# Strassen's scheme for the projection of four of twelve tiles: seven half-size products in place of eight

## The chip, the cores and the metric

The kernel runs on one NeuronCore of a Trainium2 chip. The metric is the device time of one execution in microseconds. Five engines run side by side, each with its own instruction queue: TensorE (PE, matmuls), VectorE (DVE), ScalarE (ACT), GpSimd (POOL) and SyncE (SP, which issues most DMAs). The profile's name PEld is PE's weight load, which overlaps its matmuls.

## The reference

Two steps. First attention over 4 sequences, 8 heads, 768 positions and 64 dimensions a head; some heads ("retrieval") see the whole causal past, the others a window of 64 positions and 4 sinks. Then a feed-forward layer over the 3072 resulting tokens:

```python
def _moe_ref(x, w_in, w_out) -> np.ndarray:
    h = x @ w_in              # 3072 x 512 @ 512 x 2048
    g = h - np.tanh(h)
    return (g @ w_out).astype(np.float32)   # 3072 x 2048 @ 2048 x 512
```

`x` is the attention's output with its heads side by side. Inputs and output are fp32.

## The kernel before

**Tiles.** The 3072 tokens are 12 tiles of 256 (`TT`); tiles 0 to 2 are sequence 0, and so on. Each tile goes through attention, then H (times `w_in`, tanh shrink), then O (the projection, times `w_out`). Products are fp16 with fp32 sums in the PSUM banks, of which there are eight.

**Attention.** Inputs are loaded as fp32 (`load_raw`), POOL casts and sorts the heads (`gather`, lines 641 and 677), DMAs transpose q and k, PE computes scores (`st_S`, line 1069), ACT takes the exponential (line 1082), DVE masks it (`mask`, lines 1105 and 1133), PE multiplies by v (`st_A`, line 1162), DVE normalises (line 1194), and one DMA transposes the tile into `xT` (`st_X_tile`, line 1226). In `mask`, the heads of a "near" pair (tile `ptn`) take two multiplications of 512 elements, one for each head.

**H.** `H_unit(t, u)` makes two of the 16 blocks of 128 of the hidden layer: 8 matmuls of 256 columns (line 1273) into one bank, the tanh on ACT (line 1285), and on DVE the difference, scaled, into the fp16 tile `gt` (line 1292). Eight units make a tile. There are three `gt` buffers.

**O.** `O_group` multiplies 128 tokens by `w_out`: 16 matmuls of 512 columns that sum over the 16 hidden blocks (line 1331), so 32 matmuls a tile. `store` copies the bank out on ACT (line 1305; for one half of the last tile on DVE, line 1309) and sends it (line 1317), two stores of 256 KB a tile.

**Order.** The instructions are not issued as the code writes them. Each `op(engine, ns, fn, r, w)` is recorded with a price and with keys that it reads and writes; `Plan.run` simulates the engines with these prices and issues the instructions in the simulated order, the earliest recorded first among those that are ready. A flag `port=True` marks DVE instructions that the plan delays while POOL is at work. The recording order comes from `slots`: one slot for each H unit, with a piece of the projection of the tile before, and attention steps, loads (`LD`), gathers (`GA`) and masks spread over the slots by the tables `CUT`, `CUT1` and by `spread_over`. For tiles from `QUART` = 7 on, the projection of the tile before stands in two whole groups, at units 3 and 7. After the last tile's H come its two groups of O, the second cut into two halves of 256 columns, on two queues.

`program(True)` is what runs; `program(False)` is a second version that only runs when more than four heads are retrieval heads, which isn't so here.

## Time and profile before

| | |
|---|---|
| Time of the runs | 231.74 us median of 3 (231.14 to 231.82) |
| Profiled execution, first to last instruction (span) | 229.3 us; what lies around it is 2.4 us against the median of the runs (its own whole time is not listed apart) |
| O on PE, line 1331 | 464 matmul records, 304 of 512 and 160 of 256 columns |
| H on PE, line 1273 | 768 matmuls of 256 columns |
| DVE busy | 143.7 us, of it 65.1 in line 1292, 12.7 in line 1105, 12.1 in line 1133 |
| ACT busy | 141.7 us, of it 57.3 in line 1285, 15.1 in line 1305 |
| POOL busy | 98.2 us, all of it before 155 us |
| HBM | 27.26 MB read, 6.29 MB written |

The first tanh of tile 6 begins at 124.1 us of the span, of tile 8 at 159.8, of tile 9 at 173.0, of tile 10 at 189.5, of tile 11 at 205.3; the last matmul ends at 225.25.

In the profile a line such as L1331 is a line of the kernel's file. A group's busy time is the union of its instructions, so that the mean of one, times the count, can be more. Matmuls are pipelined: a record's length is longer than the step from one to the next. The chain that ended last is followed back from the last instruction, at each step to what released it.

### The profile page before, as it was taken

What the parts mean: (1) busy time and instruction counts of PE and PEld (TensorE: products, weight loads), DVE (VectorE), ACT (ScalarE), POOL (GpSimd) and SP (SyncE); (2) the same over time, 40 slices, a digit from 0 to 9 for tenths busy, and PEclk for the clock granted to TensorE, in tenths of its full rate; (3) what the DMA queues carried; (4) which work ended last, traced back from release to release, by engine and by line L of the source; (5) the groups of instructions that cost most, each with busy time, mean ns of one, the idle gap of its engine ahead of it and who ended that gap; (6) DMA issues with size and microseconds to landing.
All of it is one profiled execution on the core that took longest, in us unless ns stands there. A gap on an engine that the chain in (4) does not pass through costs nothing.

```text
span 229.3 us, 6150 instructions
## 1 busy us (share of the span) xinstructions
PE 220.8 (96%) x2335; PEld 158.2 (69%) x2335; DVE 143.7 (63%) x350; ACT 141.7 (62%) x219; POOL 98.2 (43%) x231
## 2 busy tenths in 40 slices
PE   7889999999999999999999999999999999999992
PEld 7456687788986667767667668756857757766662
DVE  5888957875676956749655759467876546634400
ACT  3739839977477757736737757755767567433420
POOL 8999343764843839391827773370000000000000
PEclk9999999999999999999999999999999999999999
DMA  6999999999999999989999999953121301320112
GB/s 171 151 181 203 202 192 222 218 185 243 222 179 232 168 245 218 187 199 229 239 192 278 181 210 166 212 124 95 54 40 46 92 3 46 73 55 15 49 67 78
DMA packets 102964, 35.31 MB, mean 154 GB/s; under 512 B 90642, under 2 KB 100114, under 8 KB 102930
## 3 DMA queue, kind: packets, MB, share of 16 engines
q1 hardware_dynamic: 85632, 27.14, 57.0%
q0 software_dynamic: 17152, 7.60, 25.5%
q8 instruction: 19, 0.31, 0.6%
q14 instruction: 15, 0.12, 0.2%
q10 hardware_dynamic: 146, 0.13, 0.2%
HBM read 27.26 MB, written 6.29 MB: 146 GB/s over the span
## 4 chain that ended last, share of the span: by engine, by line
PE 79%; DMA 9%; POOL 5%; ACT 3%; DVE 1%; issue 1%; SPq 0%; POOLq 0%
PE banks L1331 35%; PE banks L1273 32%; DMA win<-in_moe_w_in_dram 7%; PE banks L1162 6%; PE banks L1069 6%; DMA rawqk<-in_k_dram 2%; POOL v L495 2%; ACT pt L1082 1%; POOL win L608 1%; POOL t16p L528 1%; ACT QK L955 1%; POOL A L742 0%; DVE pt L1123 0%; ACT th L1285 0%; DVE ptn L1105 0%
## 5 line engine op out<-in xcount | busy, mean ns | idle before, releaser
L1331 PE MATMUL banks<-wout,gt 128*128 128x512 f16 (+1 forms) x464 | 94.9, 343 | 0.0
L1273 PE MATMUL banks<-xT,win 128*128 128x256 f16 x768 | 93.9, 273 | 0.6 <-DVE gt L1292 0.5
L1292 DVE SCALAR_TENSOR_TENSOR gt<-th,banks 128x512 f16<-128x512 f32 x96 | 65.1, 682 | 31.3 <-ACT th L1285 30.4
L1273 PEld LDWEIGHTS <-win 128*128 128x128 f16 x768 | 73.1, 98 | 16.6 <-issue 1.7
L1285 ACT ACTIVATE th<-banks 128x512 f32<-128x512 f32 x96 | 57.3, 603 | 36.4 <-PE banks L1273 35.8
L1331 PEld LDWEIGHTS <-gt 128*128 128x128 f16 x464 | 42.4, 98 | 27.4 <-issue 1.2
L1082 ACT ACTIVATE pt<-banks 128x768 f16<-128x768 f32 (+1 forms) x60 | 53.0, 922 | 11.0 <-PE banks L1069 10.6
L641 POOL CAST t<-rawqk 128x256 f16 x72 | 28.6, 446 | 31.6 <-DMA rawqk<-in_k_dram 26.8
L1305 ACT ACTIVATE ot<-banks 128x512 f32<-128x512 f32 (+1 forms) x28 | 15.1, 538 | 24.2 <-PE banks L1331 23.5
L1194 DVE TENSOR_TENSOR x16t<-banks,rinv 128x128 f32 (+1 forms) x80 | 22.6, 287 | 1.6
L1105 DVE TENSOR_TENSOR ptn<-ptn,mS 128x512 f16<-128x512 f16 x24 | 12.7, 567 | 16.2 <-ACT ptn L1082 16.2
L1069 PE MATMUL banks<-QK 64*128 64x128 f16 (+1 forms) x364 | 21.0, 238 | 0.8 <-ACT QK L955 0.8
L677 POOL CAST v<-rawv 128x128 f16 x72 | 19.6, 322 | 0.0
L1069 PEld LDWEIGHTS <-QK 64*128 64x128 f16 x364 | 12.6, 94 | 10.0 <-issue 7.2
L1082 ACT ACTIVATE ptn<-banks 128x1024 f16<-128x1024 f32 (+1 forms) x18 | 17.1, 950 | 3.5 <-DVE x16t L1194 2.4
L1162 PEld LDWEIGHTS <-pt 128*128 128x128 f16 x420 | 16.0, 97 | 3.8 <-ACT pt L1082 0.8
L1162 PE MATMUL banks<-v,pt 128*128 128x65 f16 x220 | 16.3, 193 | 0.1
L1133 DVE TENSOR_TENSOR pt<-pt,m4r 128x1024 f16<-128x1024 f16 (+1 forms) x18 | 12.1, 673 | 5.2 <-ACT pt L1082 5.0
L1162 PE MATMUL banks<-vf,pt 128*128 128x65 f16 x200 | 13.1, 193 | 0.2 <-ACT pt L1082 0.2
L1182 DVE RECIPROCAL rinv<-banks 128x4 f32<-128x4 f32 x48 | 8.1, 174 | 5.4 <-PE banks L1162 4.7
L666 POOL COPY kc<-QK 128x128 f16<-128x128 f16 x12 | 4.1, 340 | 13.4 <-DMA QK<-t 13.3
L1162 PEld LDWEIGHTS <-ptn 128*128 128x128 f16 x132 | 6.5, 97 | 2.4 <-DVE ptn L1105 0.2
(80 smaller groups left out, 136.1 us busy)
## 6 DMA issues: line engine op xcount, KB each, us to landing
out_dram<-ot SPq DMA_DIRECT2D x19, 256.0 KB, 2.8
rawqk<-in_q_dram SPq DMA_DIRECT2D x18, 256.0 KB, 3.8
rawqk<-in_k_dram SPq DMA_DIRECT2D x18, 256.0 KB, 4.1
rawv<-in_v_dram SPq DMA_DIRECT2D x16, 256.0 KB, 4.5
win<-in_moe_w_in_dram POOLq DMA_DIRECT2D x4, 512.0 KB, 10.9
wout<-in_moe_w_out_dram POOLq DMA_DIRECT2D x4, 512.0 KB, 13.2
out_dram<-ot SPq DMA_DIRECT2D x9, 128.0 KB, 3.7
v<-in_v_dram POOLq DMA_DIRECT2D x6, 128.0 KB, 9.1
```

Of the source, the lines that this page charges most:

```text
L641: nc.gpsimd.tensor_copy(out=c5()[:, :, :, s_ : s_ + 1, :], in_=r5()[:, :, :, at, :])
L677: nc.gpsimd.tensor_copy(out=v1s[b]()[:, g * NB : g * NB + NB, RANK[s_] : RANK[s_] + 1, 0:D], in_=rv()[:, :, at, :],)
L1069: nc.tensor.matmul(out=sc()[:, hh, o : o + nb * 128], lhsT=lhsT, rhs=QK[p_, hp, q_0 : q_0 + nb * 128], start=not added, stop=not added or ...
L1082: lambda pt=pt, sc=sc, gi=gi, wid=wid: nc.scalar.activation(out=pt()[:, :, 512 * gi : 512 * gi + wid], in_=sc()[:, :, 0:wid], func=AF.Exp, ...
L1105: nc.vector.tensor_mul(out=pv, in0=pv, in1=m[:, 384:640].unsqueeze(1).to_broadcast([128, 2, 256]),)
L1162: nc.tensor.matmul(out=av()[:, i, hh, :], lhsT=pt()[:, hh, co : co + 128], rhs=vv, start=(jb == first_jb), stop=(jb == qb),)
L1194: nc.vector.tensor_mul(out=xt()[:, :, at, :], in0=av()[:, :, hh : hh + 1, 0:D], in1=rinv()[:, :, hh : hh + 1].unsqueeze(3).to_broadcast([1 ...
L1273: nc.tensor.matmul(out=ph()[:, j, :], lhsT=w_in_t[fb // 4][:, cb, f0 : f0 + 128], rhs=xT()[:, :, cb, :], start=(cb == 0), stop=(cb == HP - 1),
L1285: lambda: nc.scalar.activation(out=th()[:], in_=ph()[:], func=AF.Tanh, scale=1.0 / XS),
L1292: lambda: nc.vector.scalar_tensor_tensor(out=gt()[:, u * FU : (u + 1) * FU, :], in0=th()[:], scalar=-XS, in1=ph()[:], op0=ALU.mult, op1=AL ...
L1305: nc.scalar.activation(out=ot()[:, c0:c1], in_=po()[:, c0:c1], func=AF.Copy, scale=1.0 / XS)
L1331: nc.tensor.matmul(out=po()[:, c0:c1], lhsT=gt()[:, f, ts * 128 : ts * 128 + 128], rhs=w_out_t[:, f, c0:c1], start=(f == 0), stop=(f == NF ...
```

## The change

For tiles 8 to 11 (`ST` = 8) the product of `g` (256 x 2048) and `w_out` (2048 x 512) is taken as a 2 x 2 product of blocks: 128 tokens, every second hidden block, 256 columns. In place of eight block products there are seven, by Strassen's scheme in Winograd's form.

* **Weight sums.** Four sums and differences of the quarters of `w_out` are made once on DVE (`quads`, `combine`), in 40 instructions of 256 elements a partition: 32 spread over the slots from the first of tile 6 to the first of tile 8, the last 8 (which write over a quarter of `w_out` itself) in a slot of tile 9. They lie in a new tile `t2`, in buffers of tiles that are done with, and in `w_out`.
* **Sums of g.** For each of the four tiles DVE makes four sums of 1024 elements (`sums`), into the space of the masks `m4`.
* **Products.** `piece` is one block product: 8 matmuls of 256 columns. `step` places them in the slots of the next tile's H: products 1 and 4, 2 and 6, then 5, then 3 and 7; two of them share a bank.
* **Results.** ACT copies products out (`take`), DVE adds a product to what is there (`fold`), POOL adds three halves a tile (`add`), and two stores send 256 columns of all 256 tokens each (`send`). The last tile has an order of its own (`finale`), with its adds on DVE.
* **Tokens of tile 9.** H of tile 9 reads its tokens with a stride of two (`mixed`), so that the two halves are even and odd tokens.
* **Others.** Two `gt` buffers and one for tile 2 alone (`gu`) in place of three; the two mask multiplications of a near pair in one instruction; `CUT1` and `GA` are changed, and the prices of the masks. The second program loads `w_out` and its masks anew.

```diff
-        rawqk=2, rawv=2, t16=2, t16p=1, kc=2, pt=3, ptn=2, x16=3, x16t=2, gt=3, xT=3,
+        rawqk=2, rawv=2, t16=2, t16p=1, kc=2, pt=3, ptn=2, x16=3, x16t=2, gt=2, gu=1, xT=3,
...
+    NC = NFB // 2
+    CM = DM // 2
+    t2_t = w_pool.tile([128, NC, CM], FP16, name="t2")
...
-        gt=([128, NFB, TT], FP16), xT=([128, NB, HP, 128], FP16), th=([128, 2, TT], FP32),
+        gt=([128, NFB, TT], FP16), gu=([128, NFB, TT], FP16), xT=([128, NB, HP, 128], FP16), th=([128, 2, TT], FP32),
...
-    CUT1 = (-9.0, -7.0, 2.25, 16.0)
+    CUT1 = (-9.0, -5.0, 2.25, 13.0)
...
+    ST = 8
+    TQ = 8
+    TG = 3
+    SH = 1
+    TWHEN = ((6, 0), (8, 0), (9, 1))
+    STEPS = {1: (1, 4, "a"), 3: (2, 6, "e"), 5: (5, "b"), 7: (3, 7, "f")}
...
-    GA = 9
+    GA = 8
...
-                        for hh in range(2):
-                            pv = p_[:, hh, 0:512].rearrange("p (r c) -> p r c", r=2)
-                            nc.vector.tensor_mul(
-                                out=pv, in0=pv,
-                                in1=m[:, 384:640].unsqueeze(1).to_broadcast([128, 2, 256]),
-                            )
...
+                        pv = p_[:, :, :].rearrange("p a (r c) -> p (a r) c", r=2)
+                        nc.vector.tensor_mul(
+                            out=pv, in0=pv,
+                            in1=m[:, 384:640].unsqueeze(1).to_broadcast([128, 4, 256]),
+                        )
+
+                op("DVE", 600 if g == 0 else 740, fn, r=pk + ["mS"], w=pk, port=True)
...
+        def gt_buf(t):
+            tag = "gu" if t == 2 else "gt"
+            return (*buf(tag), tag)
+
+        def quick(t):
+            return first and t >= ST
+
+        def mixed(t):
+            return quick(t) and t % NG == 0
...
-                gts[t] = buf("gt")
-            gt, ig = gts[t]
+                gts[t] = gt_buf(t)
+            gt, ig, tag = gts[t]
...
+                        x = xT()[:, :, cb, :]
+                        if mixed(t):
+                            x = x.rearrange("p i (a two) -> p two i a", two=2)
                         nc.tensor.matmul(
                             out=ph()[:, j, :], lhsT=w_in_t[fb // 4][:, cb, f0 : f0 + 128],
-                            rhs=xT()[:, :, cb, :], start=(cb == 0), stop=(cb == HP - 1),
+                            rhs=x, start=(cb == 0), stop=(cb == HP - 1),
...
-                    "PE", 4 * 109, mm,
+                    "PE", 4 * (113 if mixed(t) else 109), mm,
...
-                r=[key, ("th", it)], w=[("gt", ig, u)],
+                r=[key, ("th", it)], w=[(tag, ig, u)] + ([("at", t)] if u == 0 else []),
...
+        S4 = [
+            m4[:, 2 * i : 2 * i + 2, :].rearrange("p a (b c) -> p (a b) c", c=128)
+            for i in range(4)
+        ]
+
+        def W_(f, m):
+            return w_out_t[:, f::2, m * CM : (m + 1) * CM]
+
+        def T_(k):
+            if k == 1:
+                return W_(0, 1)
+            if k == 2:
+                return t2_t[:]
+            if k == 4:
+                return packed[2][0]()[:].rearrange("p (c m) -> p c m", c=NC)
+            return gts[2][0]()[:, 0:NC, :]
+
+        every = [("wout", x, y) for x in range(2) for y in range(2)]
+
+        def combine(k, h, fn, a, b, w=lambda: ()):
+            cs = slice(h * NC // TQ, (h + 1) * NC // TQ)
+            op(
+                "DVE", 90 + 760 * 2 // TQ,
+                lambda: getattr(nc.vector, fn)(
+                    out=T_(k)[:, cs, :], in0=a()[:, cs, :], in1=b()[:, cs, :]
+                ),
+                r=every + [("T", x, h) for x in range(1, 5) if x != k] + [("at", TG)],
+                w=[("T", k, h), *w()], port=True,
+            )
...
+        def quads():
+            return [
+                lambda x=x, h=h: combine(x[0], h, *x[1:])
+                for x in (
+                    (2, "tensor_sub", lambda: W_(1, 1), lambda: W_(0, 1)),
+                    (2, "tensor_add", lambda: T_(2), lambda: W_(0, 0)),
+                    (
+                        4, "tensor_sub", lambda: W_(1, 0), lambda: T_(2),
+                        lambda: [("t16p", packed[2][1], x) for x in range(2)],
+                    ),
+                    (
+                        3, "tensor_sub", lambda: W_(1, 1), lambda: W_(0, 1),
+                        lambda: [("gu", gts[2][1], u) for u in range(NFU)],
+                    ),
+                    (
+                        1, "tensor_sub", lambda: W_(0, 1), lambda: W_(0, 0),
+                        lambda: [("wout", 1, y) for y in range(2)],
+                    ),
+                )
+                for h in range(TQ)
+            ]
...
+        def sums(t):
+
+            gt, ig, tag = gts[t]
+            A = lambda i, f: gt()[:, f::2, i * 128 : (i + 1) * 128]
+            g_ = [(tag, ig, u) for u in range(NFU)]
+            for k, fn, a, b, r in (
+                (0, "tensor_add", lambda: A(1, 0), lambda: A(1, 1), []),
+                (1, "tensor_sub", lambda: S4[0], lambda: A(0, 0), [0]),
+                (3, "tensor_sub", lambda: A(0, 1), lambda: S4[1], [1]),
+                (2, "tensor_sub", lambda: A(0, 0), lambda: A(1, 0), []),
+            ):
+                for h in range(SH):
+                    cs = slice(h * NC // SH, (h + 1) * NC // SH)
+                    op(
+                        "DVE", 90 + 690 // SH,
+                        lambda k=k, fn=fn, a=a, b=b, cs=cs: getattr(nc.vector, fn)(
+                            out=S4[k][:, cs, :], in0=a()[:, cs, :], in1=b()[:, cs, :]
+                        ),
+                        r=g_[h * NFU // SH : (h + 1) * NFU // SH] + [("S", x, h) for x in r],
+                        w=[("S", k, h)] + ([("m4", x) for x in range(HP)] if t == ST else []),
+                        port=True,
+                    )
...
+        def piece(t, p, beside=None):
+
+            gt, ig, tag = gts[t]
+            A = lambda i, f: lambda c: gt()[:, 2 * c + f, i * 128 : (i + 1) * 128]
+            W = lambda f, m: lambda c: W_(f, m)[:, c, :]
+            T = lambda k: lambda c: T_(k)[:, c, :]
+            S = lambda k: lambda c: S4[k - 1][:, c, :]
+            lhs, rhs, r = {
+                1: (A(0, 0), W(0, 0), []), 2: (A(0, 1), W(1, 0), []),
+                3: (S(4), W(1, 1), summed(3)), 4: (A(1, 1), T(4), both(4)),
+                5: (S(1), T(1), summed(0) + both(1)),
+                6: (S(2), T(2), summed(1) + both(2)),
+                7: (S(3), T(3), summed(2) + both(3)),
+            }[p]
+            po, key = outs[t, p] = outs[t, beside] if beside else bank(
+                [128, DM], FP32, "one", f"p{t}_{p}"
+            )
+            at = CM if beside else 0
+            for c0 in range(0, NC, 4):
+
+                def mm(c0=c0):
+                    for c in range(c0, c0 + 4):
+                        nc.tensor.matmul(
+                            out=po()[:, at : at + CM], lhsT=lhs(c), rhs=rhs(c),
+                            start=c == 0, stop=c == NC - 1,
+                        )
+
+                op(
+                    "PE", 4 * 109.3, mm,
+                    r=r + [(tag, ig, c) for c in range(c0, c0 + 4)], w=[key],
+                )
...
+        def unit(t, x):
+            if x == "A":
+                return lambda: gts[2][0]()[:, NC : NC + 4, :].bitcast(FP32).rearrange(
+                    "p a b -> p (a b)"
+                ), None
+            if ("ot", t, x) not in outs:
+                outs["ot", t, x] = buf("ot")
+            return outs["ot", t, x]
...
+        def take(t, p, x, col, wide):
+
+            po, key = outs[t, p]
+            w = own(t, x) + at_(t, x, col, col + wide)
+            ot = unit(t, x)[0]
+            op(
+                "ACT", 110 + 0.95 * wide,
+                lambda: nc.scalar.activation(
+                    out=ot()[:, col : col + wide], in_=po()[:, 0:wide], func=AF.Copy,
+                    scale=1.0 / XS,
+                ),
+                r=[key], w=w,
+            )
...
+        def fold(t, p, y, ycol, x, col, wide=DM):
...
+            def fn():
+                i_, o_ = po()[:, 0:wide], ot()[:, col : col + wide]
+                y_ = yt()[:, ycol : ycol + CM]
+                if wide > CM:
+                    i_, o_ = (z.rearrange("p (a b) -> p a b", b=CM) for z in (i_, o_))
+                    y_ = y_.unsqueeze(1).to_broadcast([128, 2, CM])
+                nc.vector.scalar_tensor_tensor(
+                    out=o_, in0=i_, scalar=1.0 / XS, in1=y_, op0=ALU.mult, op1=ALU.add
+                )
+
+            op("DVE", 160 + 1.04 * wide, fn, r=[key] + at_(t, y, ycol, ycol + CM), w=w)
...
+        def add(t, eng, fn, o, a, b):
...
+            op(
+                eng, {"POOL": 760, "DVE": 420}[eng],
...
+        def send(t, x, lo, hi, dst, ring="SP"):
...
+            how = "(r two) m -> r two m" if mixed(t) else "(two r) m -> r two m"
+            rows = out[t * TT : (t + 1) * TT, :].rearrange(how, two=2)
...
+            dma(ring, 420, go, 128, (hi - lo) * 0.18, r=at_(t, x, lo, hi) + [("ot", io)])
...
+        def columns(i):
+            return lambda rows: rows[:, :, i * CM : (i + 1) * CM]
...
+        def step(t, i):
+
+            for what in STEPS.get(i, ()):
+                if what == "a":
+                    take(t, 1, "A", 0, DM)
+                elif what == "e":
+                    fold(t, 2, "A", 0, "E", 0)
+                elif what == "b":
+                    take(t, 5, "A", 0, CM)
+                    add(t, "POOL", "tensor_add", ("E", CM), ("E", CM), ("A", 0))
+                    add(t, "POOL", "tensor_sub", ("A", CM), ("A", CM), ("A", 0))
+                elif what == "f":
+                    fold(t, 3, "E", CM, "F", 0)
+                    send(t, "F", 0, DM, columns(1))
+                    add(t, "POOL", "tensor_add", ("E", CM), ("F", CM), ("A", CM))
+                    send(t, "E", 0, DM, columns(0))
+                else:
+                    piece(t, what, {4: 1, 6: 2, 7: 3}.get(what))
...
+        def finale(t):
+
+            piece(t, 1)
+            take(t, 1, "A", 0, CM)
+            piece(t, 2)
+            fold(t, 2, "A", 0, "E", 0, CM)
+            send(t, "E", 0, CM, lambda rows: rows[:, 0, 0:CM])
+            piece(t, 4)
+            take(t, 4, "F", 0, CM)
+            piece(t, 5)
+            take(t, 5, "A", CM, CM)
+            piece(t, 6)
+            fold(t, 6, "A", 0, "E", CM, CM)
+            add(t, "DVE", "tensor_add", ("A", CM), ("A", CM), ("E", CM))
+            add(t, "DVE", "tensor_add", ("F", 0), ("F", 0), ("E", CM))
+            piece(t, 7)
+            fold(t, 7, "F", 0, "F", 0, CM)
+            fold(t, 7, "A", CM, "F", CM, CM)
+            send(t, "F", 0, DM, lambda rows: rows[:, 1, :])
+            piece(t, 3)
+            fold(t, 3, "A", CM, "E", CM, CM)
+            send(t, "E", CM, DM, lambda rows: rows[:, 0, CM:DM], "ACT")
...
+            for hp in range(HP):
+                masks(hp)
+            for i in range(4):
+                load_w_out(*divmod(i, 2))
...
+                    (("S", t - 1, u),) if quick(t - 1)
+                    else (("O", t - 1, u // 4, u % 4 * 4, u % 4 * 4 + 4, 0, DM),) if t < QUART or not first
                     else (("O", t - 1, u // 4, 0, NFB, 0, DM),) if u % 4 == 3 else ()
...
+            qs = quads()
+            spread_over(qs[: 4 * TQ], slot_of[TWHEN[0]], slot_of[TWHEN[1]])
+            spread_over(qs[4 * TQ :], slot_of[TWHEN[2]], slot_of[TWHEN[2]])
...
-            if first and fast and s == min(SPLIT, point(2 * NG * FLEX - LEAD - 1)):
+            if first and fast and s == point(2 * NG * FLEX - LEAD - 1):
...
+                    if quick(x[1] - 1) and x[2] == 0:
+                        sums(x[1] - 1)
+                elif x[0] == "S":
+                    step(*x[1:])
...
-        O_group(last, 0, 0, NFB)
-        O_group(last, 1, 0, NFB, 0, half, "DVE", "SP")
-        O_group(last, 1, 0, NFB, half, DM, "ACT", "ACT")
+        if quick(last):
+            sums(last)
+            finale(last)
+        else:
+            O_group(last, 0, 0, NFB)
+            O_group(last, 1, 0, NFB, 0, half, "DVE", "SP")
+            O_group(last, 1, 0, NFB, half, DM, "ACT", "ACT")
```

36 lines of the change are left out of this document (32 added, 4 removed).

## The prediction

> **What bounds the kernel now.** I read the page first, for shares and the clock.
>
> ```profile
> span 229.3 us, 6150 instructions
> PE 220.8 (96%) x2335; PEld 158.2 (69%) x2335; DVE 143.7 (63%) x350; ACT 141.7 (62%) x219; POOL 98.2 (43%) x231
> PEclk9999999999999999999999999999999999999999
> PE 79%; DMA 9%; POOL 5%; ACT 3%; DVE 1%; issue 1%; SPq 0%; POOLq 0%
> ```
>
> TensorE (PE) is busy 96% of the span, its granted clock stands in the top tenth throughout, and it carries 79% of the chain that ended last. Busy time alone does not prove a bound, since matmuls overlap, so I went on to the chain in order of time, from 160 us to the end.
>
> ```profile
> 171.58 0.43 PE banks L1331 x2
> 172.01 3.49 PE banks L1273 x32
> 175.50 0.72 PE banks L1069 x18
> ...
> 200.92 3.45 PE banks L1331 x16
> 204.37 3.49 PE banks L1273 x32
> ...
> 214.81 10.41 PE banks L1331 x64
> 225.23 0.02 issue
> 225.25 0.38 ACT ot L1305
> ```
>
> Each piece starts where the one before it ends: 200.92 + 3.45 = 204.37, 204.37 + 3.49 = 207.86. Between 160 and 225 us no other engine is on the chain. So in the stretch that the change shortens the end is set by how many columns PE streams, and one microsecond less on PE is one microsecond off the time, as long as the other engines keep up. They do now, as the list of waits shows:
>
> ```profile
> DVE gt L1292 <- ACT th L1285: 30.4, 51, 3.6
> PE banks L1273 <- DVE gt L1292: 0.5, 1, 0.5
> ```
>
> VectorE (DVE) waits 30.4 us for the tanh; PE waits for DVE once, 0.5 us. How near DVE is to turning this round I read from the busy times by stage. The stages begin with the first tanh of tile 6, of tile 8, 9, 10 and 11.
>
> ```profile
> core 0: us, PE busy (x) PEld busy (x) DVE busy (x) ACT busy (x) POOL busy (x), PEclk, DMA share, GB/s
> 124.10:159.80 35.70, 35.65 (x385) 24.35 (x383) 23.69 (x59) 23.18 (x36) 19.61 (x55) 1.00 0.91 172
> 159.80:173.00 13.20, 13.20 (x146) 9.97 (x145) 10.09 (x24) 9.12 (x16) 0.00 (x0) 1.00 0.17 42
> 173.00:189.50 16.50, 16.50 (x170) 11.34 (x169) 9.43 (x19) 11.24 (x17) 0.00 (x0) 1.00 0.17 49
> 189.50:205.30 15.80, 15.80 (x149) 10.94 (x146) 8.52 (x21) 8.51 (x14) 0.00 (x0) 1.00 0.21 52
> 205.30:225.30 20.00, 19.91 (x136) 13.01 (x133) 5.92 (x9) 6.60 (x12) 0.00 (x0) 1.00 0.17 60
> ```
>
> DVE has 12.0 us idle in tiles 6 and 7, 3.1 in tile 8, 7.1 in tile 9 and 7.3 in tile 10. GpSimd (POOL) works 19.6 us in the first stage and not at all after it. The change trades PE time for DVE time, so these idle times are what it spends.
>
> **The matmuls.** Now a tile's projection is 32 matmuls of 512 columns; the chain's 16 of them take 3.45 us, 215.6 ns each, 6.90 us a tile. The last tile runs 16 of these and 32 half ones: 10.41 us for tile 10's last 16 and all of tile 11 leaves 10.41 - 32 x 0.2156 = 3.51 us for the 32 halves, 109.7 ns each, so tile 11 costs 6.96 us. Afterwards each of the four tiles has 7 products of 8 matmuls with 256 columns: 56. The nearest row is H's 256-column matmul, 3.49 / 32 = 109.1 ns: 56 x 0.1091 = 6.11 us. Saved: 3 x 0.79 + 0.85 = 3.2 us. It is not a full eighth (3.5 us), since two half matmuls cost 218 ns where one whole costs 216.
>
> **The strided read of tile 9.** H of tile 9 reads every second token, so its 64 matmuls stream fp16 elements 4 bytes apart. No matmul in the trace does that. Bounds: nothing, the 109.1 ns of the contiguous row, and twice that row (+7.0 us) if only every second element read is of use. The change's own planner price is 113 instead of 109, or 0.26 us for 64. I take 0.2, near the contiguous row, because a PE stream at full rate is all the trace shows. [...]
>
> **Weight sums on DVE.** Five sums of 2048 elements a partition are cut into 40 adds of 256 fp16; 32 are spread over the slots of tiles 6 and 7, 8 stand at tile 9. The nearest rows are the mask multiplications, also fp16 with two SBUF inputs, first from 122 to 150 us, beside POOL, then from 160 to 225 us, without it:
>
> ```profile
> L1105 DVE TENSOR_TENSOR ptn<-ptn,mS 128x512 f16<-128x512 f16 x8 | 5.3, 705 | 7.8 <-ACT ptn L1082 7.8
> L1133 DVE TENSOR_TENSOR pt<-pt,m4r 128x1024 f16<-128x1024 f16 x3 | 2.2, 737 | 0.0
> ...
> L1292 DVE SCALAR_TENSOR_TENSOR gt<-th,banks 128x512 f16<-128x512 f32 x32 | 22.0, 687 | 15.4 <-ACT th L1285 14.8
> L1105 DVE TENSOR_TENSOR ptn<-ptn,mS 128x512 f16<-128x512 f16 x8 | 3.0, 422 | 5.0 <-ACT ptn L1082 5.0
> L1133 DVE TENSOR_TENSOR pt<-pt,m4r 128x1024 f16<-128x1024 f16 x4 | 2.7, 685 | 0.7 <-ACT pt L1082 0.7
> L1309 DVE TENSOR_SCALAR ot<-banks 128x256 f32<-128x256 f32 x1 | 0.4, 424 | 7.4 <-PE banks L1331 7.4
> ```
>
> Alone, 512 elements take 422 ns and 1024 take 685: 0.51 ns an element, so 256 take about 290. Consecutive DVE instructions overlap: eight of 422 ns fill only 3.0 us, the pairs lose about 0.09 us each, so one small add adds 0.20 us. Beside POOL the 512-element row is 705 ns, 0.28 more. An add so costs 0.20 (no contention) to 0.49 (the mean extra of that row): 6.4 to 15.7 us for 32. The same change merges each pair of ptn masks into one instruction; three such pairs lie in tiles 6 and 7, at 2 x 0.66 us (5.3 / 8) against 0.65 for the merged one, by the 1024-element row: 2.0 us freed. So 14.0 us are to be had up to 159.8 and 17.1 up to 173.0; the first product that reads a sum runs only in tile 9, so adds may slip into tile 8. Even at 0.49 they fit, with 1.4 us to spare. That is a 97% full engine in front of PE, so I charge for short waits of H for its banks: nothing at the low end, 1.6 us at the high end (15.7 - 14.0, if no add slips). I take the middle, 0.8, because the nearest row is the contended one. The merged masks themselves gain nothing on the path.
>
> [...] By the rows the fixed part is 0.07 us (0.20 - 256 x 0.51 ns), 35 extra instructions 2.5 us of DVE, which the sum above holds.
>
> **Sums and folds of tiles 8 to 11.** Per tile DVE gains four sums of 1024 (0.60 each by the 685 row less the overlap) and two folds like the gt row (0.60): 3.6 us. ScalarE (ACT) loses two copies and gains two, one of them half as wide. Tile 9 has besides it the last 8 adds, 1.6 us: 5.2 into 7.1 less the 0.8 by which the stage shrinks. Tile 10: 3.6 into 6.5. These hide, the first with 1.1 us of room. The POOL adds run where POOL has nothing else; what waits for them on the SP queue is a store, and behind that a transpose that has room:
>
> ```profile
> 198.44 1.24 SPq L1226 DMA_TRANSPOSE xT<-x16t  x1
> xT<-x16t SPq DMA_TRANSPOSE x10, 3.7
> ```
>
> The transpose of tile 11 is issued at 198.4, lands 3.7 later at about 202.1, and H of tile 11 starts at 204.37. If a store held it over 2.3 us, PE would wait.
>
> **Buffers and order.** Two gt buffers and one of tile 2's own instead of three: H of tile t then needs tile t-2 projected. The chain shows this already holds: tile 7's projection ends at 172.01 and H of tile 9 begins there. The shifted slots (CUT1, GA) move work among tiles that PE does without gaps; I cost them at nothing, and if a load came late they would cost that wait.
>
> **The tail.** After PE's last matmul now come a copy of 0.38 us, an issue and a 128 KB store. These rows are of the stores after 220 us:
>
> ```profile
> 225.66 0.39 ACTq L1317 DMA_DIRECT2D out_dram<-ot  x1
> out_dram<-ot SPq DMA_DIRECT2D x1, 256.0 KB, 2.0
> out_dram<-ot ACTq DMA_DIRECT2D x1, 128.0 KB, 1.8
> ```
>
> Afterwards a fold on DVE (424 ns, the L1309 row) comes last. From P6 on DVE does six dependent steps of 0.34 to 0.42, 2.0 to 2.5 us, while P7 and P3 cover 2 x 0.87 = 1.75: 0.3 to 0.8 late. A 256 KB store lands 0.2 later than the 128 KB one but is issued earlier. Bounds 0 and 0.8; I take 0.3.
>
> **Sum.** -3.2 + 0.2 + 0.8 + 0.3 = -1.9 us. The span of the profiled execution is 229.3 us, so I expect 227.4; the median of the runs is 231.74, 2.4 more for what lies around the span, which the change doesn't touch: 231.74 - 1.9 = 229.8.
>
> **Rivals.** (1) Slower: the weight adds starve H in tiles 6 to 8. If an add costs what a contended 512-element mask adds (0.66 us), 32 need 21.1 us of 17.1, H waits 4.0, and -2.7 (the sum without the crowding term) + 4.0 = +1.3, 233.0. It decides from (17.1 + 2.7) / 32 = 0.62 us an add. For it: POOL is busy 55% of the stage (19.6 of 35.7). Against it: half the elements, and the planner's own model already delays such an instruction behind POOL's (line 238). [...]
>
> (2) No change: the sums of tile 9 come late. If a sum, whose inputs are runs of 128 elements, took twice the 685 row, tile 9 would want 5.2 + 2.7 = 7.9 us of 6.3, products 5 to 7 would wait 1.6, and -1.9 + 1.6 = -0.3: 231.4. Tile 10 still fits (6.3 of 6.5). For it: DVE would already be 93% full there. Against it: the mask row, also in runs of 256, keeps full rate.
>
> (3) The strided read doubles: -1.9 - 0.2 + 7.0 = +4.9, 236.6. (4) The scheme does not do what it says, because matmuls with summed operands run slower than 109 ns; 3.2 / 4 = 0.8 us a tile over 56 matmuls is 14 ns each, and with that the sum is -1.9 + 3.2 = +1.3, 233.0. Against both: no row gives a reason.
>
> **Numbers.** Forecast 0.60 (its own range 228.6, with no crowding and no tail, to 230.9), rival 1 0.22, rival 2 0.12, rivals 3 and 4 0.06. The range leaves out rivals 3 and 4 and a part of rival 1: 228.6 to 232.9. About 0.3% (0.7 us) is what a measurement can tell from no change. Faster: 0.60 and a third of rival 2, 0.64; same: the rest of rival 2 and the mild end of rival 1, 0.10; slower 0.26.
>
> **What would show it.** Right: in the chain, 16 matmuls of a product pair take 1.75 us where 8 whole ones took 1.73, 56 a tile; no DVE on the chain between 124 and 222 us; DVE busy over 33 us of the first stage and near 14 of tile 9's; H of tile 9 at 109 to 113 ns; the time from the last matmul to the end 4.0 to 4.8 us. Wrong: PE idle before L1273 with DVE gt as releaser (rival 1), idle before products 5 to 7 with the sums as releaser (rival 2), H of tile 9 at 7 us more (rival 3).

## The result: no change that can be measured

The changed kernel takes 231.11 us (median of 20 runs, 229.75 to 233.17), the kernel before 231.34 beside it on the same chips (median of 20, 230.27 to 235.23). The ratio is 0.9992, with a 95% interval of 0.9972 to 1.0012. The forecast was 229.8, faster by 1.9 us.

The page of the changed kernel has these lines in the places of those of before:

```profile
span 230.1 us, 6393 instructions
PE 218.0 (95%) x2415; PEld 166.1 (72%) x2415; DVE 165.4 (72%) x406; ACT 141.5 (62%) x220; POOL 107.7 (47%) x240
PE 74%; DMA 10%; DVE 4%; ACT 4%; POOL 2%; issue 2%; SPq 1%; POOLq 0%; DVEq 0%
```

PE is busy 2.8 us less, and yet the span is 0.8 us longer than before's 229.3. PE's share of the chain fell from 79 to 74%, and what took its place is spread over DMA, DVE and ACT. (This execution took 231.91 us, 0.8 above its kernel's median, so its span overstates the kernel by as much.) To find where the time went I cut both traces at the same event, the first tanh of tile 8, since the scheme's products only run behind it. Each row is the timeline of ACT around it, the first of before, the second of after, with start and length in us:

```profile
159.78 0.60 ACT L1285 ACTIVATE th<-banks 128x512 f32<-128x512 f32 x1
```

```profile
162.06 0.60 ACT L1306 ACTIVATE th<-banks 128x512 f32<-128x512 f32 x1
```

From there to the end of the span it is 229.3 - 159.8 = 69.5 us before and 230.1 - 162.1 = 68.0 after: the part with the scheme became 1.5 us shorter. The part ahead of it became 2.3 us longer (about 1.5 if this execution's excess of 0.8 all fell there), although PE does the same matmuls there. So two things need an explanation: why the second part gains 1.5 us and not 3, and why the first part loses anything.

**The second part.** The chain of after in order of time, 160 us to the end:

```profile
174.06 1.81 PE banks L1294 x16
175.88 1.75 PE banks L1474 x16
...
209.91 6.99 PE banks L1294 x64
216.90 5.69 PE banks L1474 x52
...
222.78 0.48 DVE ot L1528 x2
223.26 0.19 issue
223.45 0.41 DVE gu L1539
...
224.12 1.08 DVE ot L1528 x3
```

L1294 is H, L1474 the seven products. Up to 222.6 PE stands on the chain without a break, and 16 product matmuls take 1.75 us (109.4 ns each), as forecast. Behind that the chain leaves PE for DVE: the folds and adds of the last tile. The timeline shows that the last matmul starts 6.03 us before the end of the span (224.05 of 230.1), where it was 4.33 us before (224.94 of 229.3). Of these 1.70 us, 0.45 lie ahead of the last store: the last fold ends 1.14 us after that matmul starts (225.19), the last copy before ended 0.69 after (225.63). The rest is the landing of the last stores. The rows list the DMA issues from 221 to 231 us (queue, KB each, median us to landing), to be held against the 2.0 and 1.8 of before:

```profile
out_dram<-ot SPq DMA_DIRECT2D x1, 256.0 KB, 3.2
out_dram<-ot SPq DMA_DIRECT2D x1, 128.0 KB, 3.5
out_dram<-ot ACTq DMA_DIRECT2D x1, 128.0 KB, 3.0
```

The last store is the same as before (ACT's queue, 128 rows of 256 fp32), and lands in 3.0 us in place of 1.8.

**The first part.** The chain by line between 60 and 160 us, of after:

```profile
by line: PE banks L1294 33.5%; PE banks L1352 30.0%; DMA xT<-x16t 12.3%; PE banks L1170 6.6%; PE banks L1078 6.1%; DMA QK<-t 3.2%; DVE ptn L1113 2.2%; SPq L570 1.8%; ACT th L1306 1.2%; ACT ptn L1091 1.0%; DVE gt L1313 0.7%; issue 0.5%; SPq 
```

The transposes into `xT`, which H reads, and those of q and k now carry 15% of it. In before's chain of the same stretch no landing of either has a share:

```profile
by line: PE banks L1273 41.4%; PE banks L1331 36.8%; PE banks L1069 8.3%; PE banks L1162 7.2%; DMA rawqk<-in_k_dram 4.4%; DVE ptn L1105 0.8%; SPq L597 0.6%; SPq L1226 0.5%; issue 0.1%
```

The list of PE's waits in after and its timeline say what came of it:

```profile
PE banks L1294 <- DMA xT<-x16t: 1.4, 2, 0.8
...
PE banks L1170 <- DVE ptn L1113: 0.4, 1, 0.4
...
PE banks L1078 <- DMA QK<-t: 0.4, 1, 0.4
```

```profile
89.77 0.61 PE L1294 MATMUL banks<-xT,win 128*128 128x256 f16 x4 [0.84 <-DMA xT<-x16t]
141.32 0.61 PE L1294 MATMUL banks<-xT,win 128*128 128x256 f16 x4 [0.51 <-DMA xT<-x16t]
```

PE waits for the transposes of tiles 4 and 7, 1.4 us in two places; in before's list of waits there is no such line. With the 0.4 us for a transpose of q and k, at 71 us, and the 0.4 for a merged mask, at 133 us, this is all of the 2.1 us that PE stands still between 60 us and tile 8; before it was 0.05. The chain of after shows what stands ahead of tile 7's transpose:

```profile
130.98 2.19 DVE ptn L1113
...
135.24 6.03 DMA xT<-x16t
```

L1113 is the merged mask. The median of its twelve is 0.69 us; this one took 2.2.

**The weight sums** are not where the prediction had them. The five groups of adds (first and last start in us):

```profile
L1392 DVE TENSOR_TENSOR t<-wout x8: 277/284/394, 69.8 to 71.9; 128x256 f16<-128x256 f16 x8
L1392 DVE TENSOR_TENSOR t<-t,wout x8: 277/282/470, 72.1 to 78.7; 128x256 f16<-128x256 f16 x8
L1392 DVE TENSOR_TENSOR t16p<-wout,t x8: 275/276/409, 79.1 to 83.7; 128x256 f16<-128x256 f16 x8
L1392 DVE TENSOR_TENSOR gu<-wout x8: 276/446/1202, 86.4 to 93.7; 128x256 f16<-128x256 f16 x8
L1392 DVE TENSOR_TENSOR wout<-wout x8: 280/282/282, 175.0 to 178.1; 128x256 f16<-128x256 f16 x8
```

The first four were recorded in the slots of tiles 6 and 7, yet ran at 70 to 94 us, in tiles 3 and 4. The planner issues what is ready, and a place late in the record only makes an instruction yield to earlier ones. All that holds the adds back is the key `("at", TG)` with `TG` = 3, the first unit of tile 3.

### The profile page after: what moved, and what is told of

Same layout as the page of the kernel before. It is cut to its first block, busy times and chain, and to the rows that moved or that the text cites. A ratio compares the mean times of both kernels' runs of the same rounds, so it can differ in the third digit from the quotient of the medians.

```text
span 230.1 us, 6393 instructions
## 1 busy us (share of the span) xinstructions
PE 218.0 (95%) x2415; PEld 166.1 (72%) x2415; DVE 165.4 (72%) x406; ACT 141.5 (62%) x220; POOL 107.7 (47%) x240
## 4 chain that ended last, share of the span: by engine, by line
PE 74%; DMA 10%; DVE 4%; ACT 4%; POOL 2%; issue 2%; SPq 1%; POOLq 0%; DVEq 0%
PE banks L1294 30%; PE banks L1352 21%; PE banks L1474 10%; PE banks L1170 6%; PE banks L1078 6%; DMA xT<-x16t 5%; DMA t16p<-in_k_dram 3%; ACT pt L1091 2%; DMA QK<-t 1%; DVE ptn L1113 1%; ACT th L1306 1%; POOL v L504 1%; SPq L570 1%; DVE QK L966 1%; DVE ot L1528 1%
## 5 line engine op out<-in xcount | busy, mean ns | idle before, releaser
L1294 PE MATMUL banks<-xT,win 128*128 128x256 f16 x768 | 95.1, 273 | 1.8 <-DMA xT<-x16t 1.4
L1294 PEld LDWEIGHTS <-win 128*128 128x128 f16 x768 | 72.7, 98 | 18.0 <-DMA xT<-x16t 2.8
L1313 DVE SCALAR_TENSOR_TENSOR gt<-th,banks 128x512 f16<-128x512 f32 x88 | 59.4, 680 | 19.8 <-ACT th L1306 19.1
L1352 PE MATMUL banks<-wout,gt 128*128 128x512 f16 (+1 forms) x288 | 57.4, 332 | 0.0
L650 POOL CAST t<-rawqk 128x256 f16 x72 | 29.3, 455 | 32.6 <-DMA rawqk<-in_k_dram 22.4
L1352 PEld LDWEIGHTS <-gt 128*128 128x128 f16 x288 | 25.9, 98 | 13.8 <-issue 1.2
L1539 POOL TENSOR_TENSOR ot<-ot,gu 128x256 f32<-128x256 f32 x6 | 5.3, 882 | 55.5 <-ACT gu L1509 41.3
L1113 DVE TENSOR_TENSOR ptn<-ptn,mS 128x1024 f16<-128x1024 f16 x12 | 10.8, 899 | 10.0 <-ACT ptn L1091 10.0
L1326 ACT ACTIVATE ot<-banks 128x512 f32<-128x512 f32 (+1 forms) x20 | 10.4, 520 | 6.2 <-PE banks L1352 5.4
L1474 PEld LDWEIGHTS <-m 128*128 128x128 f16 x128 | 12.2, 98 | 1.6 <-issue 0.2
```

What stands on the lines that cost most here:

```text
L650: nc.gpsimd.tensor_copy(out=c5()[:, :, :, s_ : s_ + 1, :], in_=r5()[:, :, :, at, :])
L1113: nc.vector.tensor_mul(out=pv, in0=pv, in1=m[:, 384:640].unsqueeze(1).to_broadcast([128, 4, 256]),)
L1294: nc.tensor.matmul(out=ph()[:, j, :], lhsT=w_in_t[fb // 4][:, cb, f0 : f0 + 128], rhs=x, start=(cb == 0), stop=(cb == HP - 1),)
L1313: lambda: nc.vector.scalar_tensor_tensor(out=gt()[:, u * FU : (u + 1) * FU, :], in0=th()[:], scalar=-XS, in1=ph()[:], op0=ALU.mult, op1=AL ...
L1352: nc.tensor.matmul(out=po()[:, c0:c1], lhsT=gt()[:, f, ts * 128 : ts * 128 + 128], rhs=w_out_t[:, f, c0:c1], start=(f == 0), stop=(f == NF ...
L1474: nc.tensor.matmul(out=po()[:, at : at + CM], lhsT=lhs(c), rhs=rhs(c), start=c == 0, stop=c == NC - 1,)
```

## The experiments

Three suspects were left: the weight adds in their real place, the slots of `CUT1` and `GA`, and the end of the kernel. The table has all runs. "Ratio" is to the kernel before on the same chip, where its median was between 230.94 and 231.51 us, so ratios are compared and not medians. "To 8" is the time from the start of the span to the first tanh of tile 8, "8 to end" from there to the end of the span, and "end" from the start of the last matmul to the end of the span, all in us and from the one profiled execution. Up to that tanh PE starts 1746 or 1748 matmuls; in e4 and e8, with other work around it, 1720 and 1730, so these two are compared in neither column.

| kernel | median us | ratio (95%) | to 8 | 8 to end | end |
|---|---|---|---|---|---|
| before | 231.34 | 1 | 159.8 | 69.5 | 4.3 |
| after | 231.11 | 0.9992 (0.9972 to 1.0012) | 162.1 | 68.0 | 6.0 |
| e1 no scheme | 231.75 | 1.0029 (0.9997 to 1.0061) | 160.5 | 69.3 | 4.3 |
| e2 scheme for 8 to 10 only | 231.23 | 1.0012 (0.9982 to 1.0041) | 161.0 | 67.5 | 4.7 |
| e3 no weight adds | 230.83 | 0.9995 (0.9959 to 1.0031) | 161.0 | 68.0 | 6.0 |
| e4 adds in tile 6 | 234.49 | 1.0130 (1.0088 to 1.0171) | 160.9 | 71.8 | 6.4 |
| e5 old slots | 229.74 | 0.9949 (0.9930 to 0.9969) | 160.2 | 68.3 | 6.1 |
| e6 own end buffer | 231.27 | 1.0005 (0.9981 to 1.0029) | 161.1 | 68.0 | 6.0 |
| e7 e5 and e6 | 229.61 | 0.9938 (0.9914 to 0.9962) | 159.6 | 68.2 | 6.0 |
| e8 before, new slots | 232.17 | 1.0049 (1.0028 to 1.0070) | 160.4 | 71.0 | 4.3 |
| e9 e7, product 6 first | 229.84 | 0.9917 (0.9888 to 0.9947) | 159.8 | 68.1 | 5.9 |
| e10 e2 and e5 | 229.86 | 0.9921 (0.9894 to 0.9947) | 160.6 | 67.7 | 4.6 |
| e11 old `CUT1` only | 230.23 | 0.9944 (0.9913 to 0.9976) | 161.0 | 68.0 | 5.8 |
| e12 old `GA` only | 231.57 | 0.9981 (0.9945 to 1.0018) | 163.0 | 68.0 | 6.1 |
| e13 e7 without F's store | 228.55 | 0.9886 (0.9843 to 0.9928) | 159.1 | 67.3 | 5.1 |
| e14 before, end bunched | 232.07 | 1.0030 (1.0000 to 1.0061) | 159.5 | 70.1 | 4.9 |

**e1, the change without its scheme.**

```diff
-    ST = 8
+    ST = 12
-            spread_over(qs[4 * TQ :], slot_of[TWHEN[2]], slot_of[TWHEN[2]])
```

> All of the change but the scheme: tiles 8 to 11 are projected by 32 matmuls of 512 columns as before; the first 32 weight sums are still made (and not used), the buffers, the merged masks and the slots are the changed ones. Its order of instructions is that of the changed kernel up to the first tile that the scheme projects. Theory A (what the change does ahead of tile 8 costs PE about 1.5 to 2.4 us of idle time, and the scheme earns it back): 231.3 + 1.5 to 2.4 = 232.8 to 233.7 us, with PE gaps of half a microsecond or more between 60 and 145 us. Rival B (nothing is lost ahead of tile 8, and the scheme itself saves next to nothing): 231.3 us, no such gaps.

It is 0.29% above before, where the whole change is level, and its 231.75 us lies between the times of its two theories. So the scheme gives about 0.9 us by the ratios (1.3 by "8 to end"), and the other edits take about as much away; the intervals of the two ratios overlap, so the 0.9 alone would be no proof. PE waits for the transposes of tiles 4 and 7 here too, 1.2 us without the scheme.

**e2, the scheme without its last tile.**

```diff
-            return first and t >= ST
+            return first and ST <= t < NTT - 1
```

> The scheme for tiles 8 to 10 alone; the last tile is projected and stored as before. Theory C (the scheme's own end of the kernel costs 1.4 us: 5.8 us from the last matmul to the end against 4.05 before, and a fold chain on DVE that PE doesn't cover): the last tile loses its saving of 0.85 us and wins about 1.4, so 0.5 us less than the changed kernel, about 230.6 us, with about 4.1 us from the last matmul to the end. Rival: the long end in the one profile is chance of the last stores: 0.85 us more than the changed kernel, about 232.0.

With three tiles in place of four, and the old ending for tile 11, the ratio is the same within its interval (231.23 us, between the 230.6 and 232.0 that were expected), and "8 to end" is 0.5 us shorter. The fourth tile's 0.8 us is lost again at the end.

**e3 and e4, the weight adds: none, and in tile 6.** In e3 `combine` records an empty instruction and `T_` returns plain quarters of the weight, so the order of everything else stays. e4 changes one number.

```diff
-                lambda: getattr(nc.vector, fn)(
-                    out=T_(k)[:, cs, :], in0=a()[:, cs, :], in1=b()[:, cs, :]
-                ),
+                lambda: None,
```

> The 40 weight sums are left out (the products take quarters of the weights in their place, so the output is another); every other instruction is the same and in the same order, as the planner still counts the sums. Theory A1 (the sums, which the profile shows at 69.8 to 93.7 us, contend with GpSimd's gathers, and the gathers, the queue of transposes behind them and PE run late): 1.5 us less than the changed kernel, about 229.6, gathers from tile 5 on as early as before the change, no PE gap over 0.3 us between 60 and 145 us. Rival A2 (the order, the buffers or the transfers make the gaps, the sums do not): the time of the changed kernel, 231.1, gaps as there.

```diff
-    TG = 3
+    TG = 6
```

> The weight sums may not start before tile 6 (TG 6 in place of 3), which is where the prediction had put them. By the prediction's own sum they cost 0.8 us there, and if they cost nothing at tile 3 the time is that of the changed kernel + 0.8 = 231.9; if by theory A1 they cost 1.5 us at tile 3, it is 0.7 less, 230.4. By the prediction's first rival (DVE becomes the bound beside GpSimd) it is 2 us or more above the changed kernel, 233 or later, with PE waiting for DVE between 124 and 160 us.

Without the adds the ratio is 0.9995 in place of 0.9992: where they run, they cost nothing that shows (each interval reaches 0.2 to 0.4% to either side). Held back to tile 6 they cost 3.2 us by the ratios (1.0130 - 0.9992). The busy times from e4's first tanh of tile 6 to that of tile 7 and its list of PE's waits show how:

```profile
126.30:145.00 18.70, 17.25 (x173) 11.67 (x171) 18.44 (x51) 11.40 (x17) 13.75 (x34) 1.00 1.19 198
PE banks L1352 <- DVE gt L1313: 1.6, 2, 1.2
PE banks L1170 <- DVE ptn L1113: 0.9, 1, 0.9
```

DVE (the third pair) is busy 18.44 of 18.70 us, and PE waits for `gt` and for a mask. This is the prediction's rival 1 at the place where the prediction looked for it. The change escapes it because the adds run elsewhere.

**e5 and e8, the slots.** e5 is the change with the old slots, e8 the kernel before with the new ones.

```diff
-    CUT1 = (-9.0, -5.0, 2.25, 13.0)
+    CUT1 = (-9.0, -7.0, 2.25, 16.0)
-    GA = 8
+    GA = 9
```

> The changed kernel with the slots of before (CUT1 and GA back); its order is that of the changed kernel up to 66 us. In every profile of a kernel with the changed slots so far, without the scheme and without the sums too, PE stands still for 0.8 to 1.1 us at 88 us, ahead of tile 4's H, where the kernel before has no gap. Theory D (the changed slots make that gap): no gap over 0.3 us at 82 to 95 us, and about 1.0 us less than the changed kernel, 230.1. Rival E (the buffers, the merged masks or the time of the loads make it): the gap stays, 231.1.

> The kernel before with only the changed slots (CUT1 and GA). Theory D: PE stands still for about 1 us at 88 us, and the time is 1 us or more above the kernel before, 232.3 or later. Rival E: no gap there; the time stays at 231.3, or differs for other gaps than that one.

Both answer alike. The old slots make the change faster, 0.9949 in place of 0.9992, which is 1.0 us; the new slots alone make the kernel before slower by 0.49%, 1.1 us. The chain by line from 60 to 160 us of e5, then of e8:

```profile
by line: PE banks L1294 43.6%; PE banks L1352 37.2%; PE banks L1078 8.3%; PE banks L1170 7.1%; ACT pt L1091 1.2%; issue 1.2%; ACT th L1306 0.6%; ACT ot L1326 0.5%; ACT ptn L1091 0.4%
```

```profile
by line: PE banks L1273 37.3%; PE banks L1331 34.9%; PE banks L1069 7.3%; PE banks L1162 7.0%; DMA xT<-x16t 6.2%; DMA QK<-t 3.2%; SPq L561 1.8%; ACT th L1285 0.6%; DVE gt L1292 0.6%; issue 0.5%; SPq L597 0.4%; SPq L1317 0.2%; DVE rinv L1182
```

With the old slots the transposes leave the chain of e5; with the new ones they enter it in a kernel that has nothing of the scheme. In e8 PE waits 0.9 us for a transpose of q and k at 71 us and 0.3 us for the transpose of tile 4, not the 1 us at 88 that was expected. Where they come late can be read from the rows of the transposes between 60 and 150 us, whose last start is tile 7's, of before, after, e5 and e8:

```profile
L1226 SPq DMA_TRANSPOSE xT<-x16t x5: 1244/1445/1961, 60.9 to 133.0; - x5
```

```profile
L1234 SPq DMA_TRANSPOSE xT<-x16t x5: 1716/2412/4272, 60.4 to 135.2; - x5
```

```profile
L1234 SPq DMA_TRANSPOSE xT<-x16t x5: 1554/2147/2529, 60.7 to 133.0; - x5
```

```profile
L1226 SPq DMA_TRANSPOSE xT<-x16t x5: 1237/2567/4868, 60.3 to 135.2; - x5
```

It is 133.0 with the old slots in both kernels and 135.2 with the new ones in both. Over all runs it lies at 132.7 to 133.5 with both old slots, and at 133.7 to 135.2 with both new ones (137.7 in e4); e11 and e12 below, with one of each, have 134.1 and 136.6. What PE loses by it is less clear-cut. In e9 and e10 below, with the old slots, it still waits 0.5 us for the transpose of tile 4. So the ratios show what the slots cost; that the late transposes are all of it is not shown.

The two runs with the new slots settle one thing more. e1 has every edit but the scheme and the strided read that belongs to it, e8 the slots alone, and their ratios, 1.0029 and 1.0049, are not told apart. So the buffers, the merged masks and the weight adds together add nothing that shows.

**e11 and e12, which of the two slots.** Each is the change with one of the two lines of e5's diff.

> The change with the old cuts of the second batch's attention (tiles 3 to 5), its gather still one slot later. Theory C (the cuts are most of the loss): PE's gaps at 70 and 89 us go (1.5 us in the change's profile), those at 132 and 140 us stay, 230.0 us or less. Theory G (the gather is most of it): the gaps at 70 and 89 us go but a later wait takes their place, or the gaps at 132 and 140 grow, 230.8 us or above.

> The change with the old place of the gather (9 slots ahead, tiles 6 on), its cuts kept. Theory C: the gaps at 132 and 140 us shrink (1.2 us in the change's profile), those at 70 and 89 us stay or grow, 230.7 us or above. Theory G: 230.0 us or less, and the gaps at 132 and 140 us are gone.

The old `CUT1` alone gives 0.9944, all that e5 gave; the old `GA` alone gives 0.9981, which is not told apart from the change's 0.9992. The two ran in the same rounds on one chip, and their medians are 230.23 and 231.57 us, 1.3 us apart, though the intervals of the ratios overlap a little. So it is `CUT1`, the cuts of the attention of tiles 3 to 5, as far as medians can say. The column "to 8" sets the pair apart too, 161.0 and 163.0, but e2 and e3, with both new slots, have 161.0 as well. Both expectations were partly off. e11's time lies between those of its two theories, and gaps at 70 and 90 us remained in it; in e12 those at 90 and 141 us grew to 1.2 and 1.1 us. The sum of an execution's gaps differs by about a us between kernels of the same slots ("to 8" from 160.5 to 162.1 with the new ones), so their places say less than the medians. How `CUT1` makes the loss, beyond the late transposes that the traces show, stays open.

**e6, e7 and e9, the end.** e6 gives the last tile's half E a buffer of its own, in mask space that is done with; e7 is e6 with the old slots; e9 takes product 6 ahead of product 5 in `finale`.

```diff
+            if (t, x) == (NTT - 1, "E"):
+                return lambda: m4r[:].bitcast(FP32).rearrange("p a b -> p (a b)")[:, 0:DM], None
```

> In the last tile the sums of the first columns go to the tile of a mask that is done with, not to one of the three output buffers, which at that point are held by the stores of tile 10. Nothing else changes, and the order is the same up to the last 4 us. Theory F (the fold of product 2 and its store wait for an output buffer, land on the end together with the last two stores, and these take 3.0 us in place of 1.8 to 2.0): the store of the first half is issued some 2 to 3 us earlier, the last two land within 2.0 to 2.5 us, DVE ends 0.3 us earlier, and the time from the last matmul's start to the end falls from 6.0 to 4.8 to 5.3 us; 230.1 to 230.4 us in all. Rival G (the six dependent DVE steps after product 6 alone make the long end): 5.7 us or more, 231.0.

> Both edits of the two runs above together: the slots of before and the end's own buffer. If theories D and F hold their savings add: 1.0 + 0.8, about 229.3 us, faster than the kernel before by 0.9%. If only one holds, 230.2; if none, 231.1.

> The kernel with the old slots and the end's own buffer (229.6 us, 5.95 us from the start of the last matmul to the end of the span), and in the last tile product 6 ahead of product 5. Then VectorE's addition into F comes one product (0.87 us) earlier and it no longer holds up the two folds that complete F, so F's 256 KB store leaves further ahead of the last store of 128 KB. Theory B (the last store lands in 3.2 us in place of 1.8 because it goes out 0.34 us after a store of twice its size): F's store goes out 0.7 us or more before the last one, the last lands in about 2.5 us, 5.0 to 5.3 us from the last matmul's start to the end, 228.9 us. Theory S (the store's own form or place makes it slow): the last store still takes 3.2 us and only VectorE's 0.3 us goes, 229.3 us.

With the buffer the first of the last three stores leaves 2.4 us ahead of the last matmul's start in place of 0.5 (220.72 of 223.08, 223.56 of 224.05), but the end stays at 6.0 us and the ratio where it was: waiting for a buffer isn't what costs. e9 didn't settle its question either. F's store still left only 0.34 us ahead of the last (222.51 and 222.85), since F is complete only with the folds of product 7, which stay next to the last fold on DVE. Its ratio of 0.9917 overlaps e7's 0.9938.

**e10, the old end with the old slots** (the edits of e2 and e5).

> The scheme for tiles 8 to 10 alone, tile 11 and the end as in the kernel before, and the old slots. If the new end costs what the traces showed (6.0 us in place of 4.5 from the last matmul's start) and the scheme's fourth tile is worth 0.85 us, this is 0.5 us faster than the change with the old slots alone: 229.2 us, with 4.5 to 4.7 us at the end. If the old end under the scheme costs as much in another way (stores of tile 10 crowding it), 229.7 us or above.

The end is 4.6 us, as expected, the ratio 0.9921 where e5 had 0.9949. The intervals overlap, so the scheme's fourth tile with its own end gains nothing that shows.

**e13 and e14, bunched stores.** e13 takes a store away from the new end, e14 puts one beside the last in the old end.

```diff
-            send(t, "F", 0, DM, lambda rows: rows[:, 1, :])
```

> The kernel with the old slots and the end's own buffer, without the last tile's 256 KB store of F (128 rows of the output are left unwritten). Everything else keeps its place. Theory B (bunching): the last 128 KB store, which has the form of the last one before, lands in 1.8 to 2.0 us in place of 3.2, 4.6 to 4.8 us from the last matmul's start to the end of the span in place of 5.95, about 1.2 us faster than with it: 228.4 to 228.6 us where that kernel takes 229.7. Theory S (something else in the new end): still about 3.2 us to land and 5.9 us at the end.

```diff
+            if t == NTT - 1 and c1 - c0 == DM:
+                held.append(go)
+            else:
+                if ring == "ACT":
+                    held.pop()([("ot", io)])
+                go()
```

> The kernel before, with one edit: the 256 KB store of the last tile's first 128 tokens is held back until the last 128 KB are ready, so that both go out together (SP and ACT). Theory B: the last two land in about 3.0 us in place of 1.8, the end grows from 4.3 to 5.5 us, 1.2 us slower than before. Theory S: the end stays within 0.4 us of 4.3, and the time that of before.

The DMA issues of the last 10 us, of e7, of e13 and then of e14:

```profile
out_dram<-ot SPq DMA_DIRECT2D x1, 256.0 KB, 3.2
out_dram<-m4r ACTq DMA_DIRECT2D x1, 128.0 KB, 3.2
```

```profile
out_dram<-m4r ACTq DMA_DIRECT2D x1, 128.0 KB, 2.3
```

```profile
out_dram<-ot SPq DMA_DIRECT2D x1, 256.0 KB, 2.8
out_dram<-ot SPq DMA_DIRECT2D x1, 128.0 KB, 2.3
out_dram<-ot ACTq DMA_DIRECT2D x1, 128.0 KB, 2.3
```

Both go the way of bunching, and neither the whole way. Without the 256 KB store beside it the last one lands in 2.3 us in place of e7's 3.2, and the end shrinks from 5.95 to 5.1; with one beside it in the old end, 2.3 in place of 1.8, and the end grows from 4.3 to 4.9. So a neighbour of 256 KB costs the last store 0.5 to 0.9 us. The rest, 0.5 us between 2.3 alone in e13 and 1.8 before, stays open.

## Why the prediction was wrong

The sum was -3.2 + 0.2 + 0.8 + 0.3 = -1.9. The runs make it about -3.2 + 0.3 + 0 + 1.7 + 1.0 = -0.2, and the medians differ by -0.23. That 231.1 lies inside the stated range, 228.6 to 232.9, is luck: it is above the 230.9 at which the forecast's own range ends, and what lies beyond that was there for rivals that did not happen.

* **The bound and the matmuls: right.** Behind 160 us PE is on the chain from piece to piece in both kernels. The seven products take 56 matmuls of 109.4 ns a tile, so the -3.2 is there, and rival 4 is out.
* **The strided read: right.** A row of 16 strided matmuls takes 1.81 us, 113.1 ns each against 109.1, or 0.26 us for tile 9's 64. The 0.2 was the author's estimate between bounds of 0 and 7.0 us; the measured 4 ns a matmul decides, and rival 3 is out.
* **The weight adds: wrong place.** The step took their recorded slots for their times. They ran in tiles 3 and 4 at no cost (e3). DVE's busy time in the stage of tiles 6 and 7, for which the prediction named over 33 us, is 24.0, as the first row shows; the second is tile 9's, 13.46 against the named 14:

```profile
125.10:162.10 37.00, 36.10 (x387) 24.40 (x385) 24.01 (x57) 23.12 (x36) 22.93 (x61) 1.00 0.88 188
175.10:191.90 16.80, 16.80 (x196) 14.32 (x195) 13.46 (x31) 11.15 (x17) 2.46 (x3) 1.00 0.26 48
```

  Had they run there, e4 shows that rival 1 would have come true, and at a lower price an add than its 0.62 us: the means of e4's four groups before tile 8 are 0.33 to 0.47 us, their medians 0.28 to 0.37. The term of 0.8 would have been far too small.
* **Sums and folds of tiles 8 to 11: right.** PE is busy for all of tile 9's 16.80 us in that row, so rival 2 is out: its time of "no change" was met for other reasons.
* **Buffers and order: the step that failed.** "The shifted slots (CUT1, GA) move work among tiles that PE does without gaps; I cost them at nothing." The condition that stands behind it, "if a load came late they would cost that wait", was the case: the slots cost 1.0 to 1.1 us (e5, e8), by the medians nearly all of it by `CUT1` (e11), and in the traces of the change the transposes of tiles 4 and 7 came late. That these waits are the whole loss is not shown. The forecast "no DVE on the chain between 124 and 222 us" failed too: a `gt` of 0.70 us at 129.2 and the merged mask of 2.19 us at 131.0 stand on it. The prediction had 0.65 us for a merged mask, and held that these masks gain nothing on the path. No run undoes the merge alone.
* **The tail: mis-sized.** 0.3 was taken, from bounds of 0 and 0.8, and 1.7 was measured: the end is 5.8 to 6.4 us in the nine kernels with the new end and `F`'s store, and 4.3 in before, e1 and e8. DVE's lateness was in bounds, at 0.45. What was missed is that the rows of 2.0 and 1.8 us for a landing came from stores that leave 1.6 us apart, while the new end sends 256 and 128 KB within 0.34 us. In e13 and e14 a neighbour of 256 KB is worth 0.9 and 0.5 us of the last store's landing; by what it delays that store, no run shows.
* **Sums.** Two of the prediction's sums are slightly off, and nothing above hangs on them. 15.7 - 14.0 is 1.7 and not 1.6. By its own terms the forecast's range is 228.7 to 231.1 and not 228.6 to 230.9.

The version to keep is the change with the old `CUT1` and `GA`. With e9's or e10's end it reaches 0.992 (intervals 0.989 to 0.995), some 1.9 us below the kernel before and faster than the change. e5, e7, e9 and e10 aren't told apart by their intervals.

## What to carry to other kernels

Price each constant of a planner that a change touches as an edit of its own, by the transfers that it moves: here two numbers of a tuple took away a third of what the new algorithm gave. In a list scheduler a recorded slot is a priority and not a time, so look for the keys that hold an instruction back before you say what it will crowd. At the end of a kernel, take a store's landing time from stores as far apart as they will be after the change: here a last store of 128 KB landed in 1.8 us with 1.65 us between it and the one ahead (before), and in 3.0 us with 0.34 (after).

## What was not expected of the hardware

* The matmuls of tile 9's H, whose streamed fp16 operand has a stride of 4 bytes, took 113.1 ns for 256 columns in after, 3.7% over the 109.1 of contiguous ones in before.
* The last 128 KB store landed in 2.7 to 3.3 us in seven kernels with the new end (after, e5, e6, e7, e9, e11, e12), where a 256 KB store leaves just ahead of it (0.34 us in after and e7), and in 2.3 us without that store (e13). In the old end it landed in 1.8 us (before, e1, e8), and in 2.3 us with a 256 KB store held back to go out beside it (e14).
* An add of 256 fp16 on DVE took 280 to 282 ns at 175 to 178 us, where POOL did nothing, and 276 to 1202 ns at 86 to 94 us, where POOL was busy 7.5 of 8.0 us.
